# Retention followed by a gated two-layer network: the first layer of later groups as 26 block products

## The chip, the cores and the metric

The kernel runs on one core of a Trainium2 chip. The metric is the device time in microseconds of one execution, the median of several runs. The engines are named as the profile names them: PE is TensorE (PEld its weight loads), DVE is VectorE, ACT is ScalarE, POOL is GpSimd, SP is SyncE, which here issues most DMAs.

## The reference

The input is a recurrent attention over 4 batches, 8 heads, 768 steps and a head size of 64. Its output, 3072 tokens of 512, goes through two matrix layers with a gate between them. All is float32.

```python
# attention, per batch and head, scale = 1/8
state = gamma * state + outer(k[t], v[t]);  y[t] = scale * q[t] @ state
x = y.transpose(0, 2, 1, 3).reshape(3072, 512)
# two layers: w_in is 512 x 2048, w_out is 2048 x 512
h = x @ w_in
sp = np.maximum(h, 0.0) + np.log1p(np.exp(-np.abs(h)))   # softplus
g = h * erf(sp)
return g @ w_out
```

## The kernel before

The first 512 tokens are done in four groups with ordinary matmuls. The other 2560 tokens are done in twenty "later groups": a chunk of 256 tokens times one half of the 2048 hidden features. In a later group both layers are multiplied in the manner of Strassen and Winograd, as seven products of blocks in place of eight. For the first layer, a block of w_in is 256 x 512 and a block of x is 256 x 128, so a product is 4 x 2 matmuls of 128x128x128. The sums of blocks of w_in are formed once, those of x once for each chunk, and the seven results are added up in PSUM and in `h`.

```python
def hidden_part(g, p):                      # product p of the first layer
    m, s = chunk_of(g), (g - G0) % 2        # s: which half of the hidden features
    ...
    bank = BK[g][0 if p in (1, 6, 7, 4) else 1]          # two PSUM banks
    for u in range(FG):                     # FG = 4
        for kk in range(2):
            nc.tensor.matmul(bank[:, u, :],
                w_in_sb[:, s, IN[a], kk, u * P : (u + 1) * P], XS[m][b][:, kk, :], ...)
    ...
    if p == 1:   nc.scalar.copy(h["11"], flat)
    elif p == 2: nc.vector.tensor_tensor(h["11"], h["11"], flat, op=ALU.add)
    elif p == 6: nc.scalar.copy(h["12"], flat)
    elif p == 7: nc.scalar.copy(h["22"], flat); nc.vector.tensor_tensor(h["22"], h["22"], other, op=ALU.add)
    elif p == 4: nc.scalar.copy(h["21"], flat)
    elif p == 3: nc.vector.tensor_tensor(h["12"], h["12"], flat, op=ALU.add)

def x_sums(g):                              # once per chunk
    for to, a, b in ((t1, b12, b11), (t2, b22, t1), (t3, b22, b12), (t4, b21, t2)):
        nc.vector.tensor_tensor(to, a, b, op=ALU.subtract)         # 128 x 256

# the loop over the later groups; every engine takes its instructions in this order
for g in range(G0, NG):
    hidden_part(g, 1); hidden_part(g, 2)
    if first: gated(g - 1)
    if put is not None:
        for step in range(3): put_part(put, step)        # result sums of a finished chunk
    hidden_part(g, 6)
    if first: sub_begin(j); sub_states(j)
    for _ in range(2): next(last_steps, None)            # sums of w_in and w_out, one at a time
    if put is not None: put_part(put, 3); put = None
    if not first: g_sums(g - 1)                          # sums of the gated blocks
    hidden_part(g, 5); hidden_part(g, 7)
    for _ in range(2): next(last_steps, None)
    if first: K_(j + 1); T(j + 1); project(g - 1, 0)
    else:     project_part(g - 1, 1)                     # second-layer product 1
    hidden_part(g, 4); hidden_part(g, 3)
    if more: sub_visit(j, g)                             # one attention block of 128 tokens
    if g + 1 < NG and (g - G0) % 2: x_sums(g + 1)
    if more:
        if j + 2 < NJ: K_(j + 2); T(j + 2)               # scale and transpose keys and queries
        if j + 3 < NJ: load(j + 3)
        j += 1
    ...                                                  # the first later group differs
    for p in (2, 4): project_part(g - 1, p)
    gate(g)                                              # Softplus, then Erf, on ScalarE
    for p in (5, 6, 7, 3): project_part(g - 1, p)
    if (g - G0) % 2 == 0: put = chunk_of(g - 1)
    ...
    gated(g)                                             # h * erf(...), two halves, on VectorE
```

The visit (`sub_visit`) ends like this; the copies are ScalarE's, the additions VectorE's:

```python
    for r in range(2):
        ...
        nc.scalar.copy(x, pp[r][:, :2, :])
        nc.vector.tensor_tensor(x[...], x[...], y, op=ALU.add)
    if c < NC - 1:
        nc.vector.tensor_tensor(state, ..., new[1], op=ALU.add)
```

The gate's buffer `E` exists once for the later groups; the second-layer products 1, 2 and 4 of group g - 1 read it, the products 5, 6, 7 and 3 read sums kept in the buffer of `h`.

Of the kernel before, what the change touches and what calls it, by code (L numbers as in the profile page):

```python
# [19 lines left out]
P = 128  # L20
# [12 lines left out]
IN = {"11": 0, "12": 1, "21": 2, "22": 3, "S3": 2, "S1": 4, "S2": 5, "S4": 6}  # L33
# [6 lines left out]


# [4 lines left out]
def kernel(  # L46
# [84 lines left out]
    w_in_sb = const.tile([P, 2, 7, 2, FG * P], F32, name="w_in_sb")  # L131
    w_out_sb = const.tile([P, 2, 7, FG, DH], F32, name="w_out_sb")

    def w_in_of(ft, kk):
        half, s, i = ft // (2 * FG), ft % (2 * FG) // FG, ft % FG
        return w_in_sb[:, s, 2 * half + kk // 2, kk % 2, i * P : (i + 1) * P]

    def w_out_of(ft):
# [6 lines left out]
    spare = [  # L145
        x[:, s, 4:7].rearrange("p a b c -> p (a b c)") for s, x in
        ((0, w_out_sb), (1, w_out_sb), (1, w_in_sb), (0, w_in_sb))
    ]
    raws = [x[:, : 2 * CE].bitcast(I64) for x in spare]
    numbers = spare[0][:, 2 * CE :].bitcast(U32)  # L150
    powers = [x[:, 2 * CE :].bitcast(U32) for x in spare[1:3]]
# [38 lines left out]
    def conversion(n):  # L190
# [8 lines left out]
            range(2) if n < 4 else (None,), (slice(2), slice(2, 4)) if n == 0 else (slice(None),)  # L199
        )  # L200
        for part, rows in parts:
            last = n > 0 or rows.start == 2
            words = raws[place[n]].bitcast(U32)
            if which == "in":
                f = slice(at * 2 * P, (at + 1) * 2 * P)
                if part is not None:
                    f = slice((at * 2 + part) * P, (at * 2 + part + 1) * P)
                to = w_in_sb[:, s, 2 * half : 2 * half + 2, :, f].rearrange("p d k f -> p (d k) f")
            else:
                to = w_out_sb[:, s, 2 * half : 2 * half + 2, at * 2 : at * 2 + 2, :].rearrange(  # L210
                    "p d f c -> p d (f c)"
                )
            words = words.rearrange("p (a b w) -> p a b w", a=to.shape[1], w=2)
            number, power = (
                x.rearrange("p (a b) -> p a b", a=to.shape[1]) for x in (numbers, powers[n % 2])
            )
            if part is not None:
                f = slice(part * P, (part + 1) * P)
                words, number, power = words[:, rows, f], number[:, rows, f], power[:, rows, f]
                to = to[:, rows]  # L220
            lo, hi = words[:, :, :, 0], words[:, :, :, 1]
# [25 lines left out]
    def sums(which, s):  # L247

        if which == "in":
            assert all(("hidden", 2 * FG + s * FG + u) in done for u in range(FG))  # L250
            x = {name: w_in_sb[:, s, at] for name, at in IN.items()}
            of = (("S1", "21", "22", 1), ("S2", "S1", "11", 0), ("S3", "11", "21", 0), ("S4", "12", "S2", 0))
        else:
            assert ("project", s) in done
            x = {name: w_out_sb[:, s, at] for name, at in OUT.items()}
            of = (("T1", "12", "11", 0), ("T2", "22", "T1", 0), ("T3", "22", "12", 0), ("T4", "21", "T2", 0))
        for to, a, b, plus in of:
            nc.vector.tensor_tensor(x[to], x[a], x[b], op=ALU.add if plus else ALU.subtract)
            yield
        done.add(("sums " + which, s))  # L260
# [3 lines left out]
    def weights():  # L264


        pending = [conversion(n) for n in range(n_p)]
        begun = 0
        for n, steps in enumerate(pending):
            for k, _ in enumerate(steps, start=begun):  # L270
                yield
                if n > 4 and n + 1 < n_p and k == 2:
                    next(pending[n + 1])
                    yield
            begun = int(n > 4)
            if pieces[n] == ("out", 5):
                yield from sums("in", 0)

    def later_sums():
        for which, n in (("in", 1), ("out", 0), ("out", 1)):  # L280
            yield from sums(which, n)
# [55 lines left out]
    state_1, state_2 = (const.tile([P, HP, D], F32, name=f"state{i}") for i in range(1, 3))  # L337
# [376 lines left out]
    def gate(g):  # L714


        name = "r" if g < 4 and g % 2 else "e"
        E[g] = act.tile([P, N], F32, name=name, bufs=1)
        nc.scalar.activation(E[g], HS[g], AF.Softplus)  # L719

        if g:
            gate_erf(g)
# [22 lines left out]
    def gated(g):  # L745
        for a in range(2):
            half = slice(a * N // 2, (a + 1) * N // 2)
            nc.vector.tensor_tensor(E[g][:, half], HS[g][:, half], E[g][:, half], op=ALU.mult)  # L748
        pace(-2.2)
# [67 lines left out]
    XS, BK = {}, {}  # L817
# [6 lines left out]
    def x_quarter(m, dh, th):  # L824
        at = m % 2 * SCH + th * P
        return XC[m // 2][:, 2 * dh : 2 * dh + 2, at : at + P]

    def x_sums(g):

        m = chunk_of(g)  # L830
        xs = ret.tile([P, 4, 2, P], F32, name="xs", bufs=1)
        b11, b12, b21, b22 = (x_quarter(m, d, t) for d in range(2) for t in range(2))
        t1, t2, t3, t4 = (xs[:, i] for i in range(4))
        for to, a, b in ((t1, b12, b11), (t2, b22, t1), (t3, b22, b12), (t4, b21, t2)):
            nc.vector.tensor_tensor(to, a, b, op=ALU.subtract)
        XS[m] = {"11": b11, "21": b21, "22": b22, "T1": t1, "T2": t2, "T3": t3, "T4": t4}

    def hidden_part(g, p):


        m, s = chunk_of(g), (g - G0) % 2
        if p == 1:
            HS[g] = act.tile([P, N], F32, name="h")
            BK[g] = [ps_h.tile([P, FG, P], F32, name="hp") for _ in range(2)]
        h = {name: HS[g][:, i * TCH : (i + 1) * TCH] for name, i in HQ.items()}
        a, b = PRODUCTS[p]
        if a[0] == "S":
            need("sums in", s)
        bank = BK[g][0 if p in (1, 6, 7, 4) else 1]
        for u in range(FG):  # L850
            for kk in range(2):
                nc.tensor.matmul(  # L852
                    bank[:, u, :],
                    w_in_sb[:, s, IN[a], kk, u * P : (u + 1) * P],
                    XS[m][b][:, kk, :],
                    start=(p in (1, 2, 5) and u == 0 and kk == 0),
# [3 lines left out]
        pace(1.5)  # L860
        flat = bank.rearrange("p u t -> p (u t)")
        if p == 1:
            nc.scalar.copy(h["11"], flat)
        elif p == 2:
            nc.vector.tensor_tensor(h["11"], h["11"], flat, op=ALU.add)  # L865
            pace(-0.6)
        elif p == 6:
            nc.scalar.copy(h["12"], flat)  # L868
        elif p == 7:
            nc.scalar.copy(h["22"], flat)  # L870
            other = BK[g][1].rearrange("p u t -> p (u t)")
            nc.vector.tensor_tensor(h["22"], h["22"], other, op=ALU.add)  # L872
            pace(-0.6)
        elif p == 4:
            nc.scalar.copy(h["21"], flat)  # L875
        elif p == 3:
            nc.vector.tensor_tensor(h["12"], h["12"], flat, op=ALU.add)  # L877
            pace(-0.6)
# [18 lines left out]
    def g_sums(g):  # L897
# [4 lines left out]
        for i in range(4):  # L902
            x[f"S{i + 1}"] = HS[g][:, i * TCH : (i + 1) * TCH]
        for to, a, b, plus in (
# [3 lines left out]
        G[g] = x  # L908
        pace(-2.4)
# [4 lines left out]
    def project_part(g, p, at=slice(None)):  # L914
        m, s = chunk_of(g), (g - G0) % 2
        if s == 0 and m not in O:
            O[m] = [ps_o.tile([P, 2, DH], F32, name=f"o{i}") for i in range(4)]
# [4 lines left out]
        i, half = (3, 1) if p == 4 and g >= NG - 2 else HOME[p]  # L922
        for u in range(FG):
# [10 lines left out]
        next(last_steps, None)  # L934
# [4 lines left out]
    def put_part(m, step):  # L939


        o26, o57, o34, o1 = O[m]
# [54 lines left out]
    def next_scores():  # L997
# [38 lines left out]
            ([(load, 7)], [(sub_sums, 5)]),  # L1036
            ([], [(x_sums, G0)]),
            ([], [(block_scales,)]),
# [3 lines left out]
    for g in range(G0):  # L1042
# [10 lines left out]
        if g:  # L1053
            for tt in range(TT):
# [12 lines left out]
                elif g == G0 - 1 and tt == 1:  # L1067
                    load(JPC + 4)

    j = JPC + 2
    put = None
    for g in range(G0, NG):
        first = g == G0
        more = j < NJ
        hidden_part(g, 1)
        hidden_part(g, 2)
        if first:
            gated(g - 1)  # L1080
        if put is not None:
            for step in range(3):
                put_part(put, step)
        hidden_part(g, 6)
        if first:
            sub_begin(j)
            sub_states(j)
        for _ in range(2):
            next(last_steps, None)
        if put is not None:  # L1090
            put_part(put, 3)
            put = None
        if not first:
            g_sums(g - 1)
        hidden_part(g, 5)
        hidden_part(g, 7)
        for _ in range(2):
            next(last_steps, None)
        if first:
            K_(j + 1)  # L1100
            T(j + 1)
            project(g - 1, 0)
        else:
            project_part(g - 1, 1)
        hidden_part(g, 4)
        hidden_part(g, 3)


# [11 lines left out]
        if first:  # L1120
            gate(g)
            for tt in range(1, TT):
                project(g - 1, tt)
            put_first()
        else:
            for p in (2, 4):
                project_part(g - 1, p)
            gate(g)
            for p in (5, 6, 7, 3):
                project_part(g - 1, p)  # L1130
            if (g - G0) % 2 == 0:
# [64 lines left out]
```

## Time and profile before

The median of three runs is 679.48 us (679.40 to 679.51). The profiled execution has a span of 677.6 us with TensorE at full clock throughout.

| engine | busy us | share of the span | instructions |
|---|---|---|---|
| PE | 671.8 | 99% | 6400 |
| PEld | 575.4 | 85% | 6400 |
| DVE | 392.1 | 58% | 635 |
| ACT | 257.0 | 38% | 294 |
| POOL | 7.4 | 1% | 20 |

Two neighbouring later groups, from 371.62 and from 398.43 us, last 26.81 and 26.82 us. VectorE is busy in them for 15.63 and 11.90 us: the first of the two forms the sums of x for the next chunk. A float32 matmul appears as two records on PE. A row of the timeline has the start, the length, engine, line, operation, output and inputs, the number of instructions merged, and in brackets the idle time before it with what ended it. Matmul records overlap, so a row's length has a tail of about 0.2 us; the pace is read from one row's start to the next row's.

### The profile page before, as it was taken

To read this page: it belongs to the slowest core of one execution; us is meant where nothing else is said; L and a number is where in the kernel's file an instruction comes from. 1 tells how busy PE (TensorE), PEld (TensorE's weight loads), DVE (VectorE), ACT (ScalarE), POOL (GpSimd) and SP (SyncE) were. 2 spreads that over 40 slices of the span, in tenths; PEclk is the share of its full clock that TensorE was granted. 3 is DMA by queue.
4 is the path that set the end of the run, shared out by engine and by line. 5 is a ranking of instruction groups with operands and counts; after the bars stand their busy time and mean duration, and the time that the engine had idled before them with its cause. 6 is when DMAs were issued, how large, how long until landed. Compare 5 with 4: busy or idle time off the path is not lost.

```text
span 677.6 us, 14849 instructions
## 1 busy us (share of the span) xinstructions
PE 671.8 (99%) x6400; PEld 575.4 (85%) x6400; DVE 392.1 (58%) x635; ACT 257.0 (38%) x294; POOL 7.4 (1%) x20
## 2 busy tenths in 40 slices
PE   8999999999999999999999999999999999999998
PEld 7744444668999999999999999999999999999997
DVE  5999999667845445634644553554554544333324
ACT  3477453333414415334144143242341441432430
POOL 1000000200000000000000000000000000000000
PEclk9999999999999999999999999999999999999999
DMA  9999753333423112312322321222222300000000
GB/s 188 231 254 256 178 144 77 59 61 62 119 48 75 34 32 47 76 36 43 76 41 38 76 46 31 64 44 47 69 40 45 74 2 1 1 33 1 1 32 31
DMA packets 156721, 47.67 MB, mean 70 GB/s; under 512 B 143088, under 2 KB 147568, under 8 KB 156656
## 3 DMA queue, kind: packets, MB, share of 16 engines
q1 hardware_dynamic: 156240, 46.72, 31.6%
q8 instruction: 50, 0.82, 0.5%
q14 instruction: 15, 0.12, 0.1%
q10 hardware_dynamic: 416, 0.01, 0.0%
HBM read 40.39 MB, written 6.29 MB: 69 GB/s over the span
## 4 chain that ended last, share of the span: by engine, by line
PE 98%; DMA 1%; DVE 0%; SPq 0%; ACT 0%; issue 0%
PE hp L852 37%; PE o L924 36%; PE hp L759 8%; PE o L795 8%; PE r L638 2%; PE hp L530 1%; PE o L674 1%; DMA kq<-in_k_dram 1%; PE hp L653 1%; PE r L459 1%; PE r L653 1%; PE o L506 1%; PE r L446 1%; PE r L674 0%; PE o L515 0%; PE o L499 0%
## 5 line engine op out<-in xcount | busy, mean ns | idle before, releaser
L852 PE MATMUL hp<-xs,w_in_sb 128*128 128x128 f32 x1280 | 149.7, 275 | 0.0
L852 PEld LDWEIGHTS hp<-xs,w_in_sb 128*128 128x128 f32 x1280 | 147.8, 192 | 1.5 <-issue 0.5
L924 PE MATMUL o<-w_out_sb,h 128*128 128x256 f32 (+1 forms) x648 | 142.0, 377 | 0.4 <-DVE r L1151 0.4
L924 PEld LDWEIGHTS o<-w_out_sb,h 128*128 128x128 f32 x648 | 122.3, 190 | 16.8 <-DVE r L1151 0.6
L852 PE MATMUL hp<-xT,w_in_sb 128*128 128x128 f32 x960 | 113.7, 275 | 0.0
L852 PEld LDWEIGHTS hp<-xT,w_in_sb 128*128 128x128 f32 x960 | 112.0, 192 | 1.9 <-issue 1.0
L924 PE MATMUL o<-w_out_sb,e 128*128 128x256 f32 x480 | 112.1, 383 | 0.0
L748 DVE TENSOR_TENSOR e<-h,e 128x1024 f32<-128x1024 f32 x42 | 49.5, 1221 | 100.0 <-ACT e L729 100.0
L924 PEld LDWEIGHTS o<-w_out_sb,e 128*128 128x128 f32 x480 | 88.3, 190 | 11.4
L759 PE MATMUL hp<-xT,w_in_sb 128*128 128x512 f32 (+2 forms) x144 | 56.5, 548 | 0.0
L877 DVE TENSOR_TENSOR h<-h,hp 128x512 f32<-128x512 f32 x20 | 13.8, 688 | 72.3 <-PE hp L852 72.3
L719 ACT ACT_TABLE_LOAD x24 | 30.8, 1283 | 60.8 <-issue 45.4
L759 PEld LDWEIGHTS hp<-xT,w_in_sb 128*128 128x128 f32 x144 | 25.8, 190 | 26.9 <-issue 24.6
L729 ACT ACTIVATE e<-e 128x2048 f32<-128x2048 f32 (+1 forms) x23 | 42.1, 1836 | 0.2
L719 ACT ACTIVATE e<-h 128x2048 f32<-128x2048 f32 x22 | 42.0, 1910 | 0.2
L865 DVE TENSOR_TENSOR h<-h,hp 128x512 f32<-128x512 f32 x20 | 13.7, 687 | 37.5 <-PE hp L852 37.5
L870 ACT COPY h<-hp 128x512 f32<-128x512 f32 x20 | 11.7, 586 | 61.0 <-PE hp L852 61.0
L875 ACT COPY h<-hp 128x512 f32<-128x512 f32 x20 | 11.7, 585 | 60.3 <-PE hp L852 60.3
L868 ACT COPY h<-hp 128x512 f32<-128x512 f32 x20 | 11.7, 585 | 57.1 <-PE hp L852 57.1
L692 ACT COPY xT<-r 128x256 f32<-128x256 f32 x33 | 10.8, 375 | 57.9 <-PE r L638 57.9
L729 ACT ACT_TABLE_LOAD x24 | 30.8, 1283 | 0.4
L872 DVE TENSOR_TENSOR h<-h,hp 128x512 f32<-128x512 f32 x20 | 13.8, 688 | 27.8 <-ACT h L870 27.8
(144 smaller groups left out, 667.8 us busy)
## 6 DMA issues: line engine op xcount, KB each, us to landing
w_out_sb<-in_moe_w_out_dram SPq DMA_DIRECT2D x14, 512.0 KB, 5.5
kq<-in_k_dram SPq DMA_DIRECT2D x23, 256.0 KB, 3.9
v<-in_v_dram SPq DMA_DIRECT2D x23, 256.0 KB, 3.2
out_dram<-r SPq DMA_DIRECT2D x23, 256.0 KB, 2.7
kq<-in_q_dram SPq DMA_DIRECT2D x288, 16.0 KB, 1.8
kb<-in_k_dram SPq DMA_DIRECT2D x288, 16.0 KB, 1.7
w_in_sb<-in_moe_w_in_dram SPq DMA_DIRECT2D x8, 512.0 KB, 9.5
w_in_sb<-in_moe_w_in_dram SPq DMA_DIRECT2D x8, 256.0 KB, 7.7
```

The source lines that it names most:

```text
L638: nc.tensor.matmul(pp[r][col * D : (col + 1) * D, u % 2, t], x[own, u, :], QT[j][own, u, t], start=first(r, col), stop=True, skip_group_ch ...
L653: nc.tensor.matmul(other[a][own, u % 2, D:] if crossed else pp[a][own, u % 2, t], V[j][t, 2 * u + r, :], AM[j][t, r, u, :D], start=crossed ...
L719: nc.scalar.activation(E[g], HS[g], AF.Softplus)
L729: nc.scalar.activation(E[g][:, half], E[g][:, half], AF.Erf)
L748: nc.vector.tensor_tensor(E[g][:, half], HS[g][:, half], E[g][:, half], op=ALU.mult)
L759: nc.tensor.matmul(HP_[ft][:, t], w_in_of(ft, kk), XC[0][:, kk, t], start=(kk == 0), stop=(kk == n_k - 1),)
L795: nc.tensor.matmul(O[0][tt].rearrange("p (d c) -> p d c", d=2), E[g][:, u * TCH + tt * P : u * TCH + (tt + 1) * P], w_out_of(ft), start=(f ...
L852: nc.tensor.matmul(bank[:, u, :], w_in_sb[:, s, IN[a], kk, u * P : (u + 1) * P], XS[m][b][:, kk, :], start=(p in (1, 2, 5) and u == 0 and ...
L865: nc.vector.tensor_tensor(h["11"], h["11"], flat, op=ALU.add)
L872: nc.vector.tensor_tensor(h["22"], h["22"], other, op=ALU.add)
L877: nc.vector.tensor_tensor(h["12"], h["12"], flat, op=ALU.add)
L924: nc.tensor.matmul(O[m][i][:, half, at], G[g][a][:, u * P : (u + 1) * P], w_out_sb[:, s, OUT[b], u, at], start=i not in started, stop=(s = ...
```

## The change

The first layer of a later group is no longer seven products with blocks of 256 but 26 products with blocks of 128: x is cut into 4 x 2 blocks of 128 x 128, w_in into 4 x 4 blocks of 128 x 256, and each product is two matmuls of 128x128x128. The aim is fewer matmuls: 52 in place of 56 per group. With it come:

- 30 sums of w_in blocks (128x256) for each of the two halves of the features, formed once on GpSimd; before there were four of 128x1024 for each, on VectorE.
- 18 sums of x blocks (128x128) per chunk on VectorE, in place of four of 128x256.
- 26 reads of PSUM per group: 8 copies on ScalarE (three of them with the sign turned) and 18 additions or subtractions on VectorE, each of 128x256. Four PSUM banks are used in turn, two of them those of the attention; most go on accumulating over what a bank already holds, so that a product has to wait until the bank has been read.
- Softplus of a group is issued before the visit of the same group, so it stands ahead of the visit's copies on ScalarE; Erf comes after them.
- Second-layer products 1, 2 and 4 and the result sums are placed among the 26 products.
- The staging buffers for converting the weights are laid out anew, and one attention state shares a buffer with the keys.

The core of the diff:

```diff
+W_SUMS = ((16, 2, 6, "+"), (17, 8, 10, "-"), ... )          # 30
+X_SUMS = ((0, (1, 0), (1, 1), "-"), ..., (17, 1, 15, "+"))   # 18
+STEPS = (   # w block, x block, bank, clears it?, reads (block of h, plus?)
+    (21, (1, 0), 0, True, ((4, True),)),
+    (20, 5, 1, True, ((1, False),)),
+    (10, 14, 2, True, ((3, True),)),
+    (22, 0, 3, True, ((5, True),)),
+    (23, 7, 0, False, ((5, True),)),      # h block 5 again: an addition on VectorE
+    (24, (0, 1), 1, False, ((7, False),)),
+    (25, 15, 2, False, ((2, True),)),
+    (14, (2, 1), 3, False, ((7, True),)),
+    (9, 8, 0, False, ((7, True),)),       # the ninth: bank 0 again
...                                         # 26 in all
-    w_in_sb = const.tile([P, 2, 7, 2, FG * P], F32, name="w_in_sb")
+    w_in_sb = const.tile([P, 2, N_W, 2 * P], F32, name="w_in_sb")
+    def sums_in(s):
+        for to, a, b, sign in W_SUMS:
+            nc.gpsimd.tensor_tensor(w_in_sb[:, s, to], w_in_sb[:, s, a], w_in_sb[:, s, b], op=OP[sign])
+    def hidden_steps(g):
+        HS[g] = act.tile([P, N], F32, name="h")
+        banks = [pool.tile([P, FG, P], F32, name=name) for pool, name in ((ps_h, "hp"), (ps_r, "r")) for _ in range(2)]
+        for w, x, bank, first, reads in STEPS:
+            for u in range(2):
+                nc.tensor.matmul(banks[bank][:, u, :], w_in_sb[:, s, w, u * P : (u + 1) * P], XS[m](x),
+                                 start=first and u == 0, ...)
+            for o, plus in reads:
+                if o in written: nc.vector.tensor_tensor(h, h, of, op=ALU.add if plus else ALU.subtract)
+                elif plus:       nc.scalar.copy(h, of)
+                else:            nc.scalar.activation(h, of, AF.Copy, scale=-1.0)
+            yield
-            ([(load, 7)], [(sub_sums, 5)]),
-            ([], [(x_sums, G0)]),
-            ([], [(block_scales,)]),
+            ([(load, 7), (block_scales,), (sums_in, 0)], [(sub_sums, 5)]),
+            ([], []),
+            ([], []),
 for g in range(G0, NG):
+        if first: sums_in(1); sub_begin(j); sub_states(j)
+        elif put is not None: put_part(put, 0)
+        for n, _ in enumerate(hidden_steps(g), start=1):
+            if first: ...                                   # gating, scaling and a projection in between
+            if put is not None and n in (14, 16, 18):
+                put_part(put, n // 2 - 6)
+            ...                                             # sums of the gated blocks, one or two at a time
+            if n in (14, 18, 24):
+                project_part(g - 1, {14: 1, 18: 2, 24: 4}[n])
+        gate_softplus(g)
         if more: sub_visit(j, g)
         if g + 1 < NG and (g - G0) % 2: x_sums(g + 1)
         if more:
             if j + 2 < NJ: K_(j + 2); T(j + 2)
             ...
-            for p in (2, 4): project_part(g - 1, p)
-            gate(g)
+            gate_erf(g)
             for p in (5, 6, 7, 3):
                 project_part(g - 1, p)
+                next(last_steps, None)                      # sums of w_out, in the first two later groups
```

In the first of these, three further projections of the four ordinary groups take the place of the second-layer products, and the four sums of the first half of w_out are issued between them.

## The prediction

> **What bounds the kernel now.** I read the page first: busy times, the chain that ended last, the costliest groups.
>
> ```profile
> PE 671.8 (99%) x6400; PEld 575.4 (85%) x6400; DVE 392.1 (58%) x635; ACT 257.0 (38%) x294; POOL 7.4 (1%) x20
> ...
> PE 98%; DMA 1%; DVE 0%; SPq 0%; ACT 0%; issue 0%
> ...
> L852 PE MATMUL hp<-xs,w_in_sb 128*128 128x128 f32 x1280 | 149.7, 275 | 0.0
> ...
> L852 PE MATMUL hp<-xT,w_in_sb 128*128 128x128 f32 x960 | 113.7, 275 | 0.0
> ```
>
> TensorE is busy 99% of the span and is 98% of the chain, so time saved on it is saved in full, as long as nothing makes it wait. The first layer of the later groups (L852) is 149.7 + 113.7 = 263.4 us in 1280 + 960 = 2240 records. That is 117.6 ns each with their tails; the steady pace comes from the timeline. Each float32 matmul leaves two records.
>
> Next I read TensorE's timeline over one later group.
>
> ```profile
> 398.44 0.83 PE L852 MATMUL hp<-xT,w_in_sb 128*128 128x128 f32 x6
> ...
> 402.01 5.52 PE L852 MATMUL hp<-xs,w_in_sb 128*128 128x128 f32 x48
> 407.37 1.89 PE L924 MATMUL o<-w_out_sb,e 128*128 128x256 f32 x8
> ...
> 414.79 3.72 PE L924 MATMUL o<-w_out_sb,e 128*128 128x256 f32 x16
> 418.35 7.07 PE L924 MATMUL o<-w_out_sb,h 128*128 128x256 f32 x32
> 425.25 3.73 PE L852 MATMUL hp<-xT,w_in_sb 128*128 128x128 f32 x32
> ```
>
> From start to start, 48 first-layer records take 407.37 - 402.01 = 5.36 us, so a record is 0.1117 us and a matmul 0.2235. The 48 second-layer records take 425.25 - 414.79 = 10.46, or 0.218 each, 1.745 us for a product of four matmuls. A group lasts 425.25 - 398.44 = 26.81 us: 112 x 0.1117 = 12.51 first layer, 7 x 1.745 = 12.2 second layer, and 2.0 for the attention visit (412.77 to 414.79). Nothing is left over, so TensorE never waits.
>
> Last, VectorE in the group before that and at the start of this one. These rows are what the change will disturb.
>
> ```profile
> 388.54 0.53 DVE L694 TENSOR_TENSOR xT<-xT,hp 128x128 f32<-128x128 f32 x2
> ...
> 390.44 0.42 DVE L835 TENSOR_TENSOR xs<-xT,xs 128x256 f32<-128x256 f32 x1
> 390.78 0.69 DVE L417 TENSOR_TENSOR kq<-kq,kq_s 128x512 f32<-128x512 f32 x1
> ...
> 393.21 0.67 DVE L439 STREAM_TRANSPOSE qT<-kq 128x512 f32<-128x512 f32 x1
> 398.23 2.36 DVE L748 TENSOR_TENSOR e<-h,e 128x1024 f32<-128x1024 f32 x2 [4.35 <-ACT e L729]
> 402.28 0.69 DVE L865 TENSOR_TENSOR h<-h,hp 128x512 f32<-128x512 f32 x1 [1.69 <-PE hp L852]
> ```
>
> After the visit's adds (L694), the x sums (L835) and the five scale and transpose steps (L417 to L439), VectorE is still idle for 4.35 us until Erf has ended. Then it gates, and waits 1.69 us more for TensorE. So it has some 6 us in hand when a group starts. Back to back, a 128x512 operation follows the last after 0.60 us, a 128x256 after 0.335, a 128x1024 after 1.14; on the same line a 128x128 takes 0.20. An operation that needs the result just before it comes about 0.11 later.
>
> **What the Trainium skill says.** "SBUF — State Buffer", section "Who interferes with whom": a VectorE instruction with two SBUF inputs and a GpSimd instruction that reads SBUF exclude each other for a whole instruction. The trace agrees: five tiny GpSimd products beside a full VectorE took a median of 1106 ns, about one VectorE operation each, where the 128x8 products with VectorE nearly free (L360) took 299.
>
> ```profile
> L385 POOL TENSOR_TENSOR kq_b<-kq_b,by_b x5: 570/1106/1176, 119.6 to 123.9; 128x32 f32<-128x32 f32 x5
> ```
>
> "GPSIMD Engine Reference", section 3.1, measures 4497 ns for a float32 addition of 2048 elements per partition. For 256 that scales to 562 ns; with start-up I estimate 0.65 us. No operation of that size is in the trace. "ScalarE: Activation LUTs", section "What ACT_TABLE_LOAD costs", gives about 1283 ns for a load, and the trace shows 1283. The same page's "Table sets" puts copies in every set, so the negated copies should need no load.
>
> **The change, part by part.**
>
> *Removed.* 26 products of two matmuls are 52, against 56 before. 4 x 0.2235 = 0.894 us per group, for 20 groups 17.9 us. Undisturbed, a group is 26.81 - 0.89 = 25.9 us and the kernel 679.5 - 17.9 = 661.6.
>
> *Added on VectorE.* Instead of three 128x512 additions a group has 18 of 128x256, from PSUM: 18 x 0.335 = 6.0 against 1.8, so +4.2 us. The x sums are 18 of 128x128, six of them waiting for the one before: 12 x 0.20 + 6 x 0.31 = 4.3 against 1.6, so +2.7 in every second group. The busy times of a pair of groups (15.63 + 11.90 = 27.5 us) grow to some 39 of 51.7: it fits on average. ScalarE has 8 copies of 128x256 for 4 of 128x512, about the same time.
>
> *Moved.* Second-layer products 1, 2 and 4 now lie among the 26, so TensorE's order in a group is: 26 products and three second-layer products (11.6 + 5.2 = 16.9), visit 2.0, four second-layer products 7.0. Softplus now stands in ScalarE's order ahead of the visit's copies.
>
> *What that order does to VectorE.* I follow an odd group, one that forms the x sums for the next, with its start at 0:
> - 16.9: first layer ends. Last addition 0.27 later plus 0.42: 17.6.
> - Table load 1.3 and Softplus 1.9: ScalarE is busy until 20.8. TensorE ended the visit at 18.9, but the two copies (0.65) run from 20.8 to 21.4.
> - VectorE's visit additions wait for those copies, and everything behind them too. They and the state sum end their issue near 22.0.
> - 18 x sums, 4.3: 26.3. Scales and transposes, 3.0: 29.3. Erf ended at about 24.6, so it no longer counts. Gating, 2 x 1.14: 31.6. The next group's first addition (product 5), 0.42: 32.0.
>
> TensorE starts that next group at 25.9. Products 1 to 8 need only ScalarE's copies, but product 9 accumulates in the bank of product 5 and has to wait for its addition. It would start at 25.9 + 8 x 0.447 = 29.4; with 0.15 for signal and refill it starts at 32.1. **Stall: 2.7 us in each even group that follows the x sums and the scaling.** In odd groups the same chain lacks the x sums, gating ends at about 27, and nothing waits. After the stall VectorE catches up in the 1.7 us second-layer slots. Such even groups are the 4th to the 16th after the first later group, seven: 7 x 2.7 = 18.9. The 2nd is worse: three of the w_out sums (1.14 to 1.25 each, 3.5) now stand before the gating: 2.7 + 3.5 = 6.2. In the 18th the scaling has ended, and 31.6 - 3.0 leaves no stall.
>
> *The first two later groups.* The GpSimd sums start at about 114 us (the block scales come 5 us earlier, as the first w_in sums leave VectorE). 30 x 0.65 would fit before the products that use them. But VectorE then has conversions, scales and 18 x sums in line, nearly all with two SBUF inputs. If these alternate with GpSimd, each x sum takes 0.2 + 0.6, and the 15th of them, needed by product 3 at about 129.6, comes between 129 (two slip in at a time) and 135. I take 5 us. In the following group four w_out sums (4.9) lie before the gating, behind keys that came at 154 us before: 4 us. Together 9.
>
> Sum: 679.5 - 17.9 + 18.9 + 6.2 + 9 = 695.7. I say **695.5 us**: the saving on TensorE is real, and more than given back in waits.
>
> **The rivals.**
> - *VectorE keeps up*, and the whole 17.9 us stays: 662. For it: 58% busy, and 6 us in hand at a group's start. Against it: the order, which puts 2 us of waiting, 2.7 of longer x sums and the delayed gating into one stretch.
> - *The stalls are half as long*, for instance as the scales run faster or the copies come earlier: about 12 us less, 683, and the kernel stays within 2%.
> - *GpSimd is much slower under the lock* (1.5 us an operation): then sums 9 to 28 come late as well, and the first two groups lose 20 us instead of 9: 707.
> - *26 changes of bank with a wait each cost TensorE time of their own*: 0.03 us x 26 x 20 = 16 us, 711. Against it: the 48 records above cross product boundaries with waits and still run at 0.1117.
>
> **Range and chances.** The gain is counted and sure to 1 us. The pair stall is uncertain by 0.5 us x 8 = 4, the first groups by 5, and the walk as a whole can be wrong in its order. So 686 to 704. 2% slower is 693.1, just under my middle: 0.58 for slower by over 2%, 0.35 for within. Only the first rival gives over 2% faster: 0.07.
>
> **What would show it.** L852's successor: 2080 records at 0.1117 us steps. TensorE with 25 to 35 us of idle time, most of it waiting for a first-layer addition on VectorE, every second group at the ninth product, and odd groups at 25.9 us. VectorE idle for some 2 us behind Softplus at the visit, and no longer idle before gating in odd groups. GpSimd operations at 0.6 us alone and over 1 us beside VectorE. I am wrong if even groups also last 25.9 us (the x sums or scales then end sooner than I count), or if TensorE loses time at each bank change.

## The result: 3% slower, and where the time went

The changed kernel takes 700.39 us (median; 699.63 to 702.16) against 679.44 for the kernel before: a ratio of 1.0312, 95% interval 1.0297 to 1.0327. The profiled execution has a span of 697.9 us, 20.3 more than before. First the page of the changed kernel: busy time by engine, the chain that ended last, and the two costliest groups of the first layer's matmuls.

```profile
PE 665.0 (95%) x6240; PEld 565.4 (81%) x6240; DVE 521.4 (75%) x1067; ACT 267.8 (38%) x374; POOL 63.7 (9%) x80
...
PE 63%; DVE 20%; SPq 5%; issue 4%; ACT 4%; DMA 3%; DVEq 0%; ACTq 0%
...
L949 PE MATMUL hp<-xs,w_in_sb 128*128 128x128 f32 x1040 | 151.1, 282 | 21.8 <-DVE h L961 21.1
...
L949 PE MATMUL r<-xs,w_in_sb 128*128 128x128 f32 x480 | 70.8, 287 | 4.9 <-DVE am L629 4.9
```

TensorE has 160 records fewer, as meant. But it is busy for 95% of the span where it was 99%, and VectorE now makes up 20% of the chain. The last column says where TensorE stood still: 21.1 us for additions to `h` on VectorE (L961), 4.9 us for a mask (L629). Before, that column was 0.0.

TensorE's timeline at the start of an even later group, the eighth after the first:

```profile
359.71 0.61 PE L949 MATMUL hp<-xT,w_in_sb 128*128 128x128 f32 x4
360.15 0.61 PE L949 MATMUL hp<-xs,w_in_sb 128*128 128x128 f32 x4
...
362.83 0.61 PE L949 MATMUL r<-xT,w_in_sb 128*128 128x128 f32 x4
365.45 1.31 PE L949 MATMUL hp<-xs,w_in_sb 128*128 128x128 f32 x8 [2.01 <-DVE h L961]
366.56 1.92 PE L949 MATMUL r<-xs,w_in_sb 128*128 128x128 f32 x8
```

Four records, one product, start 0.44 us after the last; so the 26 products run at full pace. The row at 365.45 is the ninth product, after 2.01 us of nothing. In the row after it, eight records take 368.27 - 366.56 = 1.71 us in place of 0.89 (the next row starts at 368.27). VectorE in the group before, which forms the x sums, shows what the ninth product waited for:

```profile
354.77 0.56 DVE L786 TENSOR_TENSOR xT<-xT,hp 128x128 f32<-128x128 f32 x2 [1.43 <-ACT xT L784]
355.25 0.41 DVE L791 TENSOR_TENSOR state<-state,r 128x256 f32<-128x256 f32 x1
355.58 1.09 DVE L931 TENSOR_TENSOR xs<-xT 128x128 f32<-128x128 f32 x5
...
359.72 0.69 DVE L509 TENSOR_TENSOR kq<-kq,kq_s 128x512 f32<-128x512 f32 x1
...
362.74 2.32 DVE L843 TENSOR_TENSOR e<-h,e 128x1024 f32<-128x1024 f32 x2
364.98 0.42 DVE L961 TENSOR_TENSOR h<-h,hp 128x256 f32<-128x256 f32 x1
```

From the copies on there is no idle time left: VectorE stands for 1.43 us until ScalarE has made the visit's copies, then it works without a gap to the addition of product 5 at 364.98. That ends at 365.40 and the ninth product starts 0.05 us later. ScalarE's line shows the copies (L784) directly behind Softplus:

```profile
352.57 1.91 ACT L811 ACTIVATE e<-h 128x2048 f32<-128x2048 f32 x1
354.39 0.63 ACT L784 COPY xT<-r 128x256 f32<-128x256 f32 x2
```

Before the change they had waited for TensorE alone:

```profile
388.10 0.65 ACT L692 COPY xT<-r 128x256 f32<-128x256 f32 x2 [3.24 <-PE r L638]
```

The slow row at 366.56 is something else. A view by windows has the length of the window, TensorE's busy time in it with the number of its records, and then the granted clock. The first of these windows of 3.41 us holds the wait:

```profile
362.90:366.31 3.41, 1.40 (x12) 1.00 0.22 34
366.31:369.72 3.41, 3.41 (x18) 0.50 0.22 34
369.72:373.13 3.41, 3.41 (x25) 1.00 0.36 82
```

The clock is at one half for 3.41 us after TensorE has stood still. Before, the mean clock was 1.000, now it is 0.985. The difference of the two spans, 20.3 us, in parts:

| part | us | from |
|---|---|---|
| 80 matmuls fewer | -17.9 | 20 x 0.894; an odd group lasts 25.92, before 26.81 |
| waits, even groups 4 to 16 | +13.7 | 2.01, 1.81, 2.01, 2.01, 1.80, 2.01, 2.00 |
| wait, group 2 | +5.4 | one of 5.41 |
| waits, first later group and group 1 | +7.7 | 4.95, 0.72, 0.51; 0.73, 0.77 |
| half clock | +8.4 | groups 8, 14, 16: 29.8 against 28.2, 1.6 each; group 2 about 2.1; first later group 1.4 |
| remainder | +3.0 | mostly the following two: a wait costs some 0.27 more than it shows as idle, 1.9 for seven (group 4 lasts 28.20; 25.92 + 2.01 = 27.93); the first later group starts at 128.65, before at 127.46 |

Groups are numbered from the first later group as 0. Idle time is counted from the end of the last record, its tail of about 0.2 us included, so the start of the next product is put off by more than the idle time.

### The profile page after: what moved, and what is told of

The parts are those of the page before. It is cut to its first block, busy times and chain, and to the rows that moved or that the text cites. A ratio compares the mean times of both kernels' runs of the same rounds, so it can differ in the third digit from the quotient of the medians.

```text
span 697.9 us, 15334 instructions
## 1 busy us (share of the span) xinstructions
PE 665.0 (95%) x6240; PEld 565.4 (81%) x6240; DVE 521.4 (75%) x1067; ACT 267.8 (38%) x374; POOL 63.7 (9%) x80
## 4 chain that ended last, share of the span: by engine, by line
PE 63%; DVE 20%; SPq 5%; issue 4%; ACT 4%; DMA 3%; DVEq 0%; ACTq 0%
PE o L1016 27%; PE hp L949 20%; PE r L949 10%; SPq L187 5%; DVE xs L931 4%; DVE e L843 2%; PE o L890 2%; DMA kq<-in_k_dram 2%; ACT e L811 1%; DVE h L961 1%; DVE w_out_sb L317 1%; DVE kb L516 1%; DVE kq L516 1%; DVE w_out_sb L325 1%; PE r L730 1%
## 5 line engine op out<-in xcount | busy, mean ns | idle before, releaser
L949 PE MATMUL hp<-xs,w_in_sb 128*128 128x128 f32 x1040 | 151.1, 282 | 21.8 <-DVE h L961 21.1
L961 DVE TENSOR_TENSOR h<-h,hp 128x256 f32<-128x256 f32 x200 | 82.5, 420 | 74.6 <-PE hp L949 71.0
L961 DVE TENSOR_TENSOR h<-h,r 128x256 f32<-128x256 f32 x160 | 61.4, 418 | 22.9 <-PE r L949 19.2
L949 PE MATMUL r<-xs,w_in_sb 128*128 128x128 f32 x480 | 70.8, 287 | 4.9 <-DVE am L629 4.9
L949 PEld LDWEIGHTS r<-xs,w_in_sb 128*128 128x128 f32 x480 | 64.0, 203 | 5.1 <-issue 5.1
L963 ACT COPY h<-hp 128x256 f32<-128x256 f32 x40 | 14.9, 373 | 128.8 <-PE hp L949 92.6
L343 POOL TENSOR_TENSOR w_in_sb<-w_in_sb 128x256 f32<-128x256 f32 x60 | 57.0, 973 | 1.9
L949 PE MATMUL hp<-xT,w_in_sb 128*128 128x128 f32 x320 | 48.9, 275 | 0.0
L854 PEld LDWEIGHTS hp<-xT,w_in_sb 128*128 128x128 f32 x144 | 25.7, 190 | 27.0 <-issue 24.6
L949 PEld LDWEIGHTS hp<-xT,w_in_sb 128*128 128x128 f32 x320 | 43.8, 192 | 1.5 <-issue 0.5
L965 ACT ACTIVATE h<-hp 128x256 f32<-128x256 f32 x60 | 23.1, 384 | 55.8 <-PE hp L949 54.4
L949 PE MATMUL r<-xT,w_in_sb 128*128 128x128 f32 x240 | 33.3, 275 | 0.0
## 6 DMA issues: line engine op xcount, KB each, us to landing
w_in_sb<-in_moe_w_in_dram SPq DMA_DIRECT2D x8, 512.0 KB, 11.3
```

The costliest lines, as they stand in the source:

```text
L343: nc.gpsimd.tensor_tensor(w_in_sb[:, s, to], w_in_sb[:, s, a], w_in_sb[:, s, b], op=OP[sign])
L854: nc.tensor.matmul(HP_[ft][:, t], w_in_of(ft, kk), XC[0][:, kk, t], start=(kk == 0), stop=(kk == n_k - 1),)
L949: nc.tensor.matmul(to[:, u, :], w_in_sb[:, s, w, u * P : (u + 1) * P], XS[m](x), start=first and u == 0, stop=True, skip_group_check=True,)
L961: nc.vector.tensor_tensor(h, h, of, op=ALU.add if plus else ALU.subtract)
L963: nc.scalar.copy(h, of)
L965: nc.scalar.activation(h, of, AF.Copy, scale=-1.0)
```

## The experiments

The theory: the waits come from the order of VectorE's queue, not from its amount of work. Between the visit's copies and the addition of product 5 lie the x sums, the scales and the gating, and Softplus holds up the copies. In the first two later groups GpSimd's sums lock VectorE out on top of that. And the clock falls because TensorE stands still. The rivals are named in each expectation.

**Softplus after the visit's copies again.**

```diff
-        gate_softplus(g)
         if more:
             sub_visit(j, g)
...
+        gate_softplus(g)
         gate_erf(g)
```

> The changed kernel with one thing undone: Softplus is issued after the visit's copies again; no work is added or left out. Theory (the order of VectorE's queue makes the stalls: visit additions wait for copies that wait for Softplus): VectorE gets to the x sums about 1.8 us earlier, the wait at the ninth product of the even groups falls from 1.8-2.0 us to 0-0.3, the long one of the second later group from 5.4 to about 3.6, the stretches at half clock after the short waits go; time 678 to 684 us. Rival (VectorE simply has too much work in the two groups): the same work, so the waits stay near 2 us, time within 2 us of 700.

Measured: 682.56 us, ratio to the kernel before 1.0044 (1.0029 to 1.0059). The copies wait for TensorE again and no longer for Softplus, and the ninth product, here of group 8, waits less:

```profile
348.12 0.65 ACT L784 COPY xT<-r 128x256 f32<-128x256 f32 x2 [9.59 <-PE r L730]
```

```profile
359.21 1.16 PE L949 MATMUL hp<-xs,w_in_sb 128*128 128x128 f32 x8 [0.46 <-DVE h L961]
```

The waits at the ninth product of groups 4 to 16 are 0.46 or 0.25 us, that of group 2 is 3.86, and none of groups 4 to 16 has a stretch at half clock any more. The same instructions in another order are 17.8 us faster (about 5 of them half clock), so the rival, the amount of work, falls. The waits did not quite go away: 2.01 to 0.46 is 1.55 us, not 1.8.

**Scales and transposes moved into the next group, Softplus left first.**

```diff
             if j + 2 < NJ:
-                K_(j + 2)
-                T(j + 2)
+                if (g - G0) % 2:
+                    late = j + 2
+                else:
+                    K_(j + 2)
+                    T(j + 2)
...                                  # in the loop over the 26 products
+            if late is not None and n == 16: K_(late)
+            if late is not None and n == 20: T(late); late = None
```

> The changed kernel, but in the groups that form x sums the scales and transposes of the next keys and queries are issued inside the next group (after its products 16 and 20) instead of before the gating; Softplus stays ahead of the copies and no work is left out. Theory (what counts is the length of VectorE's line between the copies and the addition of product 5): the line is 3.0 us shorter, so the 1.8-2.0 us waits of the even groups vanish, the one of 5.4 becomes about 2.4, and no new wait of over 0.5 us appears; time 676 to 682 us. Rival (amount of work): the waits come back later in the even groups, time 695 or more.

Measured: 675.97 us, ratio 0.9947 (0.9932 to 0.9962): 0.5% faster than the kernel before. The ninth product of group 8 starts without a wait:

```profile
355.73 1.06 PE L949 MATMUL hp<-xs,w_in_sb 128*128 128x128 f32 x8
```

No wait is left in groups 4 to 16, the one of group 2 is 2.42, and none came up elsewhere. The time was foretold as 676 to 682, and lies just below. Another 3 us out of the same line does what moving Softplus did, so it is the length of the line that counts.

**The waits filled with matmuls that nobody reads.** Real work and all waits on VectorE stay.

```diff
+            if step == 8 and (g - G0) % 2 == 0 and 2 <= g - G0 <= 16:
+                for _ in range(24 if g - G0 == 2 else 9):
+                    nc.tensor.matmul(to[:, 3, :], w_in_sb[:, s, w, :P], XS[m](x), start=False, stop=True, ...)
```

> The changed kernel with matmuls that nobody reads put into the waits: 9 (2.0 us) after product 8 of the even later groups 4 to 16, 24 (5.4 us) in the second. All real work and all waits on VectorE stay. Theory (the clock falls to one half for about 3.4 us because TensorE stood still): the clock stays at 1.0 in these groups, about 1.6 us less in each of the three even groups that had a slow stretch and 1.8 in the second, some 0.2 us more where the fill is longer than the wait; time 692 to 695 us. Rival (the slow clock has another cause, such as the load): time 699 to 702, slow stretches still there.

Measured: 693.82 us against 700.39 without the filling, 6.6 less with 87 matmuls more. The timeline shows group 8 with the filling (L961 here is the added line), and the window view shows the clock behind it:

```profile
362.21 2.17 PE L961 MATMUL r<-xT,w_in_sb 128*128 128x128 f32 x18
364.38 1.16 PE L950 MATMUL hp<-xs,w_in_sb 128*128 128x128 f32 x8
365.38 1.06 PE L950 MATMUL r<-xs,w_in_sb 128*128 128x128 f32 x8
```

```profile
365.00:370.00 5.00, 5.00 (x39) 1.00 0.29 52
```

The row behind the ninth and tenth product takes 0.89 us again (the next row starts at 366.27), and the clock is 1.00. The stretches at half clock are gone from all these groups; the one in the first later group, where nothing was filled in, is still there. So standing still is the cause. This is no gain over the kernel before (ratio 1.0211), but it separates the two costs: of the pair's loss the wait itself is the larger part.

**Without GpSimd's sums of w_in.** The kernel leaves 60 sums out and fills their places with a constant.

```diff
-        for to, a, b, sign in W_SUMS:
-            nc.gpsimd.tensor_tensor(w_in_sb[:, s, to], ...)
+        nc.gpsimd.memset(w_in_sb[:, s, 16:26], 0.01)
```

> The changed kernel without the 60 sums of w_in blocks on GpSimd: in their place two fills of the sum slots with a constant, so the later groups multiply with meaningless weights; everything else is done. Theory (GpSimd and VectorE exclude each other, which stretches VectorE's line in the first two later groups): x sums of the first later group at 0.2 us instead of 0.75, its waits of 6.2 us in all fall below 1, the 1.5 us of the next group vanish, the half-clock stretch at 135 us goes; time 690 to 693 us. Rival (VectorE's order alone makes these waits, with or without GpSimd): time 697 or more.

Measured: 695.39 us (691.78 to 697.84). The waits of the first later group fall from 6.2 to 0.51 us and its half-clock stretch goes. What the sums did to VectorE is seen in one x sum, first in the changed kernel, then without the sums:

```profile
126.41 0.81 DVE L931 TENSOR_TENSOR xs<-xT 128x128 f32<-128x128 f32 x1
```

```profile
122.34 0.29 DVE L930 TENSOR_TENSOR xs<-xT 128x128 f32<-128x128 f32 x1
```

0.81 against 0.29 us for the same operation. The 18 x sums take 11.3 us (122.56 to 133.9) with the sums, and 4.2 without. The mask that TensorE waited for stands behind them. But the time missed its 690 to 693: group 1 now has a wait of 2.10 us, where I had expected none. VectorE, no longer held up, waits there for keys:

```profile
153.99 0.69 DVE L515 TENSOR_TENSOR kb<-kb,kq_b 128x512 f32<-128x512 f32 x1 [5.13 <-DMA kb<-in_k_dram]
156.42 4.71 DVE L349 TENSOR_TENSOR w_out_sb<-w_out_sb 128x1024 f32<-128x1024 f32 x4
```

The keys land at 153.99, then come the scales and four sums of w_out, and the gating is late again. A part of what the first later group gained is given back in the next. The profile is one of the faster executions (span 690.1); the slowest of the six has a span of 696.1. Most of that difference is half clock: the mean granted clock is 0.990 in the one and 0.983 in the other, so 690.1 x 0.010 = 6.9 us are lost to it in the one and 696.1 x 0.017 = 11.8 in the other.

**The sums of w_out moved, four of them to GpSimd.** On top of the moved scales.

```diff
-                next(last_steps)                 # at the ends of groups 0 and 1
+            if g == G0 + 1 and n in (15, 16, 20, 21, 22):
+                next(last_steps)                 # four on VectorE, in group 1
...
+            sums_out_1()                         # four on GpSimd, behind its sums of w_in
```

> As e2 (scales and transposes of the groups that form x sums issued inside the next group), and the eight sums of w_out taken from the ends of the first two later groups: four on VectorE among the last products of the second of them, four on GpSimd after its w_in sums. No work is left out. Theory (VectorE's line before the gating makes the waits): the 2.42 us wait of the third later group and the half-clock stretch behind it go, and so does the 0.75 us one of the second; the 6 us of the first stay; about 4.5 us less than e2's 676.0, so 670 to 673. Rival (too much work on VectorE in these groups): the waits come back among the last products, time 675 or more.

Measured: 677.86 us, ratio 0.9975 (0.9969 to 0.9982), above the 670 to 673 expected. The wait of group 2 and that of 0.75 are gone as foretold, but group 1 has a new one of 4.10 us and one of 0.67. The reading, from VectorE's line in group 1:

```profile
172.62 1.33 DVE L1005 TENSOR_TENSOR h<-e 128x512 f32<-128x512 f32 x1
173.98 2.73 DVE L1005 TENSOR_TENSOR h<-h,e 128x512 f32<-128x512 f32 x1
176.63 4.62 DVE L350 TENSOR_TENSOR w_out_sb<-w_out_sb 128x1024 f32<-128x1024 f32 x2
...
181.84 0.69 DVE L1005 TENSOR_TENSOR h<-e 128x512 f32<-128x512 f32 x1
```

The same operation takes 1.33, 2.73 and later 0.69 us. GpSimd's four sums of 128x1024 ran from 168.60 to 178.91, and the VectorE operations with two inputs in SBUF that fell into that time are the long ones. The time and the place of the new waits are those that the rival named; whether the amount of work or the lock makes them, this run does not tell.

**The first 12 sums of w_in on VectorE.** On top of that, so that GpSimd is silent until the x sums are done.

```diff
-            ([(load, 7), (block_scales,), (sums_in, 0)], [(sub_sums, 5)]),
+            ([(load, 7), (block_scales,)], [(sub_sums, 5)]),
-                    waiting.append((x_sums, G0))
+                    waiting.extend([(x_sums, G0), (sums_in_own, slice(9))])   # VectorE
...
+            sums_in_own(slice(9, 12)); sums_in(0)       # the other 18 on GpSimd
```

> As e5, and the first 12 of the 30 w_in sums for the first later group go to VectorE, behind its x sums; GpSimd does the other 18 from then on, starting with one that needs VectorE's, so that it reads nothing while VectorE finishes the conversions and the x sums. No work is left out; VectorE has 12 operations more. Theory (beside a busy VectorE, a GpSimd sum costs VectorE 0.54 us, more than the 0.34 to 0.45 it needs to form it itself): the x sums take 4 us instead of 11, the 5 us wait at product 3 of the first later group falls to about 1, the half-clock stretch goes, 5 us less than e5, so 665 to 668. Rival (VectorE's work is what counts, wherever GpSimd stands): 12 operations more on VectorE, time as e5 or later.

Measured: 679.05 us, ratio 0.9991 (0.9984 to 0.9997), far from 665 to 668. Yet the part that was changed did as expected: the x sums take 4.2 us, the waits at the start of the first later group are 0.89 and 0.18 in place of 4.97, no half clock, and that group ends 4.6 us sooner. VectorE had 12 operations more and was done with all of them at 132.08 us, sooner than with the x sums alone in the changed kernel (133.95). All of it is lost in group 1, with waits of 0.89, 3.90 and 4.94 us and half clock. GpSimd started later, so its sums of w_out (from 172.36 us, before from 168.60) met more of VectorE's work.

**All sums of w_out on VectorE**, the first four ahead of the scaling of group 0, where it waits for keys.

```diff
             sub_visit(j, g)
+        if first:
+            for _ in range(4): next(last_steps)
...
-            sums_out_1()
```

> As e6, but the eight sums of w_out are all on VectorE again: the first four ahead of the scaling in the first later group, where VectorE waits for keys anyway, the other four among the last products of the next group. No work is left out. Theory (in e5 and e6 the large GpSimd sums, 3 us each, lock VectorE out and make the waits of 4.1, 3.9 and 4.9 us in the second later group): these waits and the half-clock stretch behind them go, at most 1 us is left there, 10 to 12 us less than e6, so 666 to 669. Rival (VectorE has too much work in the second later group, with or without the lock): waits of 3 us and more stay there, time 675 or more.

Measured: 670.58 us, ratio 0.9867 (0.9853 to 0.9882), the best of all and 8.9 us faster than the kernel before; 1.6 us above the range expected. The page's busy line and its line of the granted clock:

```profile
PE 656.9 (98%) x6240; PEld 558.1 (84%) x6240; DVE 515.3 (77%) x1079; ACT 268.1 (40%) x374; POOL 55.9 (8%) x68
...
PEclk9999999999999999999999999999999999999999
```

The waits of 3.9 and 4.9 us in group 1 are gone. VectorE has as many sums of w_out among the products of group 1 as in the run before, four, so the amount of work there is not their cause. What differs is how long it takes; one and the same operation of group 1, first in the run before, then here:

```profile
176.16 2.82 DVE L1012 TENSOR_TENSOR h<-e,h 128x512 f32<-128x512 f32 x1
```

```profile
175.29 1.21 DVE L1006 TENSOR_TENSOR h<-e,h 128x512 f32<-128x512 f32 x1
```

So the lock made these waits. TensorE is at full clock throughout, later groups last 25.92 us, and nine waits of 0.18 to 0.89 us, 6.1 in all, are left in the first two. VectorE is busier than in the changed kernel (77% against 75% of the span), and from the third later group on TensorE doesn't wait for it. Of the 17.9 us counted as saved 8.9 arrive; the nine waits and the later start of the first later group account for most of the rest.

**The same with Softplus after the visit.** The edit is that of the first experiment.

> As e7, with Softplus behind the visit's copies as in e1. Theory (the place of Softplus matters only through the wait at the ninth product, and e7 has none left): the time of e7 within 0.3%. Rival (Softplus first costs, or saves, time by itself): over 2 us apart from e7.

Measured: 670.53 us, ratio 0.9869 (0.9852 to 0.9885), the same as before the edit. Softplus has no price of its own: 17.8 us in one surrounding, none in the other.

## Why the prediction was right, and what it missed

The measured 700.4 us lie inside 686 to 704, on the side of slower by over 2% that I held most likely, 4.9 us above my 695.5. Point by point:

- *The saving.* Right: 26.81 to 25.92 us per group, and no cost for the changes of bank. The rival of 26 waits with a cost of their own falls.
- *The chain in an odd group.* Right in its order and close in time. From the group's start at 333.79: Softplus ends at 20.7 (said 20.8), x sums begin at 21.8 (22.0), scales at 25.9 (26.3), gating at 28.95 (29.3), the ninth product runs at 31.7 (32.1). Moving Softplus and moving the scales each shortened it as they should.
- *The size of the pair stall.* I said 2.7 us from start to start. Measured in the same way it is 2.1 to 2.3 (group 4 lasts 28.20 in place of 25.92), some 15.5 in place of 18.9 for the seven; 1.8 to 2.0 of each, 13.7 in all, show as idle time. The mis-sized terms are small ones: the x sums took 4.14 in place of 4.3, the end of the visit 0.2 less, the gating 0.04 less, and the start after the wait 0.05 in place of 0.15. There is a slip in my sum too: 25.9 + 8 x 0.447 is 29.5, not 29.4.
- *Group 2.* 6.2 said, 5.4 measured as idle time.
- *The first two later groups.* 9 said, 7.7 measured, but as 6.2 + 1.5 where I had 5 + 4. Here the step was partly another: I had product 3 wait for the 15th x sum. It waited for its bank, which a mask had to read that stands behind all 18 x sums. The lock was right: 0.81 us for an x sum where I took 0.8. That its removal is partly given back through the keys at 154 us was in my sum, as 4 us for group 1; the changed kernel lost 1.5 us there, and the experiment without GpSimd's sums 2.7.
- *GpSimd's operation.* 0.65 us estimated from "GPSIMD Engine Reference", section 3.1; measured were 0.72 for the shortest of the 60, 0.77 for the median, and 0.97 as a mean beside VectorE. The rival of 1.5 us falls. Only one matmul's weight load waited for a sum on GpSimd, 0.9 us.
- *The negated copies.* As said, no table load came with them: 49 loads before, 49 now.
- *Missed: the clock.* I had no term for it. The waits I had summed were 34.1 us and measured 26.8 as idle time, and the remainder in the table adds 3.0; the half clock, 8.4 us, more than made up for the difference. Without it the kernel would have taken some 692 us, just within 2% of the kernel before. So the order and the path were foretold, but that the time fell near my middle and on the side of over 2% is luck: two errors cancel. The experiment with filled waits shows the cause of most of the 8.4.

Why some waits of 2.0 us end in half clock (groups 8, 14, 16) and others don't (4, 10) can be read from the traces. The half-clock stretches of the changed kernel that follow a wait begin at 134.21, 199.06, 366.31, 530.15 and 584.76 us. They are 19, 49, 48 and 16 times 3.413 us apart, and last 3.41 us or twice that. So the clock was set in fixed steps of 3.413 us that do not start with the wait, and what counts is how long TensorE is idle within one step. In group 8 one step holds the whole wait (3.41 - 1.40 = 2.01 us idle in the first window above). In group 4 the wait falls on a border and is split into 1.43 and 0.58 us:

```profile
253.67:257.09 3.42, 1.99 (x18) 1.00 0.23 36
257.09:260.50 3.41, 2.83 (x25) 1.00 0.19 30
```

Over all traces, each step at full clock with 2.00 us of idle time or more was followed by half clock, and none with less than 1.80. Of seven between 1.80 and 1.89 one was: in the kernel without the sums on GpSimd the 1.81 us of group 12, while the 2.10 us of its group 1, split by a border into 0.28 and 1.82, had no half clock behind it. This is read off the traces; no run moved a wait against the steps on purpose. The Trainium skill, page "TensorE: Matmul & The Clock Gate", section "What's actually happening", has the clock halved after an idle window of about 3.4 us, and the window free-running. The traces agree with the length and with the fixed steps, but here the window did not have to be idle throughout: 2.0 us of it was enough.

## What to carry to other kernels

When the bounding engine is made faster, follow the queue of the engine that feeds it, in program order, from its last release to the operation that TensorE needs; a busy share of 75% does not tell whether TensorE waits (at 77%, in another order, it hardly did), and the same work in another order was worth 18 us here. Sums given to GpSimd are not free beside VectorE: a GpSimd operation that reads SBUF cost a VectorE operation with two inputs in SBUF half a microsecond, more than the 0.33 to 0.46 us in which VectorE formed a 128x256 sum itself when GpSimd was silent. And count a wait on TensorE as more than its length.

## What the runs showed of the hardware

- TensorE's clock was set in fixed steps of 3.413 us. After a step at full clock with 2.00 us of idle time or more it was at half for one to three steps (groups 8, 14, 16, and after the waits of 4.95 and 5.41 us), which costs 1.4 to 2.1 us each; after a step at full clock with less than 1.80 us idle it never was. With matmuls in the wait it didn't happen.
- The lock that "SBUF — State Buffer", section "Who interferes with whom", describes acts by whole instructions: a 128x128 addition on VectorE took 0.81 us beside 128x256 sums on GpSimd and 0.29 without, a 128x512 one up to 2.73 us beside 128x1024 sums and 0.69 without.
- Additions on VectorE with one input in PSUM did not show it: the first-layer additions beside GpSimd's sums kept their 0.42 us (137.76 to 139.76 us in the changed kernel).
